# Products of ones ahead of the first rows, and a new order for the rest rows, the split rows and one weight's conversion

## The chip, the core and the metric

The kernel runs on one core of a Trainium2 chip. Its engines are TensorE (matrix products), VectorE and GpSimd (elementwise work), ScalarE (activation functions, copies, casts) and SyncE, whose queue issues the loads. In the rows of the profile they are called PE (PEld for its weight loads), DVE, POOL, ACT and SP. Each engine runs its instructions in a fixed order and waits where an input is missing or a buffer is not yet free. [...]

The metric is the device time of one execution in microseconds, as the median of several runs. Lower is better.

## What is computed

Four batches of 6336 rows and 256 channels go through channel attention and then a gated convolution:

```python
qn = q / (np.linalg.norm(q, axis=1, keepdims=True) + 1e-06)
kn = k / (np.linalg.norm(k, axis=1, keepdims=True) + 1e-06)
s = kn.transpose(0, 2, 1) @ qn / tau
a = softmax(s)                                  # 256 x 256 per batch
x = v @ a
gate = sigmoid(sum_k conv_w[k] * x shifted by k)    # 5 taps along the rows
out = (gate * (x @ w_val)) @ w_out
```

The softmax above stands for the reference's own lines (subtract the maximum, exponentiate, divide by the sum plus 1e-9). The weights w_val, conv_w and w_out arrive as 64-bit floating-point numbers, everything else as 32-bit ones.

## The kernel before

**Scores.** The sum k^T q runs over the 6336 rows of a batch. Rows are spread over the 128 partitions, 49 to a partition, so that a "row" of the kernel (one j) is 128 rows of the matrix; 64 rows remain, the *rest* (lines 47, 48). The 49 are cut into 17 groups: the first has one row, the others three (`GROUP`, lines 63 to 65). `load_group` (line 69) fetches a group of q and of k into one of six `raw` buffers; for the first group of each batch it also fetches the rest rows.

`score_group` (line 166) prepares a group and returns its products:

- A row with j below `nw` is *raw*: TensorE multiplies the 32-bit numbers as they are (line 222). A row from `nw` on is *split*: ScalarE casts it to a shorter format (line 192), GpSimd subtracts this from the original (line 193), and TensorE forms three products of the halves in the faster format for each half of the channels (line 224).
- The squares for the norms are formed by ScalarE (line 209, into `sq`, two buffers). VectorE adds the rows with j below `nv` to an accumulator in PSUM, GpSimd adds the others to one in SBUF (lines 210 to 214). The squares of a group stand behind that group's cast on ScalarE (line 196).

In batch 0 the first eleven groups are wholly raw, with two of the three rows added by VectorE; from group `SIDE` = 11 on, the third row is split and VectorE adds all three (line 172). In batch 1 the first five groups are raw, later ones are wholly split.

**The first loop** (lines 477 to 494) runs the 17 groups of batch 0. TensorE's first instruction is the product that clears the scores in PSUM (line 231), which needs the zeros that VectorE writes at line 88. At n = 6 it issues the loads of both weights (`load_weights`, line 105) and makes two generators, `prepare_weights(0)` for w_val with conv_w and `prepare_weights(1)` for w_out. Each turns the 64-bit words into 32-bit numbers in eight or more steps on VectorE (lines 132 to 154); for w_out ScalarE also makes a cast (line 149). From n = 9 on, two steps of each follow a group. The raw words of w_val take one of the three buffers of the split halves (tag `hi`), those of w_out one of the two output buffers (tag `o_sb`). At n = 13 the loads for batch 1's first groups and for the first rows of v follow.

**After it** (lines 495 to 524) the softmax of batch 0 goes on step by step (`softmax`, line 236, one step a `tick`). Between its steps TensorE works on batch 1's first five groups and transposes v; `behind` ties a block's instructions to stand behind a marked one of the same engine. Then comes the main loop over 52 steps of 508 rows of v: `conv` (product with the attention, five taps on ScalarE and VectorE), `sigmoid`, `value` (product with attention times w_val), `split_g` and `finish` (product with w_out, line 404, the first user of its two halves).

The order of the program's lines is a priority. The compiler decides each engine's order with it, and may put a later line ahead when the inputs of an earlier one are not there yet by its own estimate.

Of the kernel before, what the change touches and what calls it, by code (L numbers as in the profile page):

```python
# [17 lines left out]
P = 128  # L18
# [4 lines left out]
SIDE = 11  # L23
# [5 lines left out]
def kernel(  # L29
# [38 lines left out]

    def load_group(b, g):
        j0, n = groups[g]  # L70
        t = raw_p.tile([P, GROUP, 2, C], F32, name="raw")
        for s, src in ((0, q), (1, k)):
            main = src[b, 0:RP * P].rearrange("(p j) c -> p j c", j=RP)
            last_load[0] = nc.sync.dma_start(out=t[:, 0:n, s, :], in_=main[:, j0:j0 + n, :])  # L74
            if g == 0 and REST:
                nc.sync.dma_start(out=t[0:REST, n, s, :], in_=src[b, RP * P:N])
        raws[b, g] = t
# [10 lines left out]
    nc.vector.memset(zeros.bitcast(F32), 0.0)  # L88
    dummy = const.tile([P, 1], F32, name="dummy")
# [76 lines left out]
    def score_group(b, g):  # L166
# [4 lines left out]
        if b == 0:  # L171
            nw, nv = (GROUP, 2) if g < SIDE else (2, 3)
        else:
            nw, nv = (GROUP, 1 if g else 2) if b == 1 and g < LEAD else (0, 2)
        parts = [(P, 0, n)]
        if g == 0 and REST:
            parts.append((REST, n, 1))
# [10 lines left out]
        sq = split_p.tile([P, GROUP, 2, C], F32, name="sq", bufs=2)  # L188
# [21 lines left out]
        for np_, j in rows:  # L210
            if j in where:
                continue
            eng, key = (nc.vector, "acc") if j < nv else (nc.gpsimd, "side")
            eng.tensor_tensor(st[key][0:np_], st[key][0:np_], sq[0:np_, j], ALU.add)  # L214

        def mms(np_, j):
            r = slice(0, np_)
            stop = g == NG - 1 and np_ == parts[-1][0] and j == parts[-1][1] + parts[-1][2] - 1
            for h in range(NH):
# [5 lines left out]
                for n_, (lhs, rhs) in enumerate(ops):  # L225
                    nc.tensor.matmul(st["s"][:, h, :], lhs, rhs, start=False,  # L226
                                     stop=stop and h == NH - 1 and n_ == len(ops) - 1)
# [203 lines left out]
    marks = {}  # L431
# [41 lines left out]
    def step(n):  # L473
        return all_steps[n] if 0 <= n < len(all_steps) else None


    for n in range(NG):
        if n == 6:
            load_weights(0)
            load_weights(1)  # L480
            prep.extend(prepare_weights(part) for part in range(2))
        if n == NG - 4:
            load_upto(NG + 1)
            with tc.issue_after(last_load[0].ins):
                load_v(*step(0))
            load_upto(NG + 3)
# [3 lines left out]
        run_group()  # L490
# [28 lines left out]
    while stages:  # L519
        tick()  # L520
    for h in range(NH):
        transpose_v(*step(1), h)
# [84 lines left out]
```

## Time and profile before

| | us |
|---|---|
| median of 3 runs | 657.92 |
| fastest, slowest run | 657.75, 658.62 |
| span of the profiled execution, first to last instruction | 653.8 |

The profile gives no time of its own for the profiled execution beyond its span; the median of the runs is 4.1 us above it.

How it stands by stage, from the busy time by stretch (each entry is busy us of that stretch):

| stretch, us | what runs | TensorE | VectorE | ScalarE | GpSimd | GB/s |
|---|---|---|---|---|---|---|
| 0 to 14 | first loads, first groups | 10.55 | 4.14 | 6.97 | 2.21 | 259 |
| 14 to 38 | groups of batch 0 | 24.00 | 20.68 | 12.20 | 11.17 | 340 |
| 38 to 46 | groups of batch 0 | 6.44 | 7.65 | 5.44 | 3.74 | 327 |
| 46 to 54 | last groups of batch 0 | 8.00 | 7.41 | 6.10 | 3.86 | 279 |
| 54 to 72 | first softmax, batch 1's first groups | 17.33 | 10.79 | 12.16 | 5.62 | 345 |
| 72 to 82 | first steps of v | 8.68 | 8.58 | 9.08 | 9.12 | 216 |
| 82 to 100 | main loop | 18.00 | 15.39 | 14.02 | 16.09 | 232 |

A busy TensorE is not one at full pace: the ends of its products are modelled, and they overlap. Its pace is read from the distance between starts, or from the count of instructions in a stretch without idle time.

### The profile page before, as it was taken

To read this page: it belongs to the slowest core of one execution; us is meant where nothing else is said; L and a number is where in the kernel's file an instruction comes from. 1 tells how busy PE (TensorE), PEld (TensorE's weight loads), DVE (VectorE), ACT (ScalarE), POOL (GpSimd) and SP (SyncE) were. 2 spreads that over 40 slices of the span, in tenths; PEclk is the share of its full clock that TensorE was granted. 3 is DMA by queue.
4 is the path that set the end of the run, shared out by engine and by line. 5 is a ranking of instruction groups with operands and counts; after the bars stand their busy time and mean duration, and the time that the engine had idled before them with its cause. 6 is when DMAs were issued, how large, how long until landed. Compare 5 with 4: busy or idle time off the path is not lost.

```text
span 653.8 us, 10657 instructions
## 1 busy us (share of the span) xinstructions
PE 636.1 (97%) x4008; PEld 570.3 (87%) x4008; DVE 521.7 (80%) x831; ACT 465.7 (71%) x607; POOL 362.1 (55%) x174
## 2 busy tenths in 40 slices
PE   7999999999999999999998999999999999999996
PEld 5878799998979999999997998999999798988886
DVE  3897689787878688778788688778778889888894
ACT  5465978867888768668688787777777755655564
POOL 2441896965837769659565497766763122312221
PEclk9999999999999999999999999999999999999999
DMA  8999875555635665545554375653222343443213
GB/s 272 336 320 335 267 233 154 152 170 162 188 99 175 186 195 176 167 136 173 177 178 127 113 222 168 179 182 103 65 80 76 113 126 102 114 129 105 65 51 99
DMA packets 107875, 105.75 MB, mean 162 GB/s; under 512 B 5744, under 2 KB 107312, under 8 KB 107824
## 3 DMA queue, kind: packets, MB, share of 16 engines
q1 hardware_dynamic: 82048, 79.76, 39.8%
q10 hardware_dynamic: 25776, 25.32, 13.7%
q8 instruction: 31, 0.51, 0.3%
q14 instruction: 20, 0.16, 0.1%
HBM read 79.11 MB, written 25.95 MB: 161 GB/s over the span
## 4 chain that ended last, share of the span: by engine, by line
PE 84%; DVE 4%; ACT 4%; DMA 3%; SPq 2%; POOL 1%; issue 1%; ACTq 0%; DVEq 0%
PE o_ps L404 21%; PE x_ps L345 19%; PE val_ps L345 19%; PE s_ps L226 17%; PE t_ps L335 6%; SPq L74 2%; DMA raw<-in_k_dram 1%; PE o_ps L294 1%; POOL hi L193 1%; DMA w_raw<-in_moe_conv_w_dram 1%; DMA v_raw<-in_v_dram 1%; ACT hi L192 1%; DVE acc_ps L214 1%; DVE gate L361 1%; DVE gate L374 1%
## 5 line engine op out<-in xcount | busy, mean ns | idle before, releaser
L361 DVE SCALAR_TENSOR_TENSOR gate<-x_ps,wa,gate 128x508 f32<-128x508 f32 (+1 forms) x416 | 275.4, 718 | 14.4 <-ACT gate L359 13.4
L193 POOL TENSOR_TENSOR hi<-raw,hi 128x1536 fp32r<-128x1536 f32 (+2 forms) x54 | 167.8, 3109 | 92.8 <-ACT hi L192 92.8
L388 POOL TENSOR_TENSOR g_lo<-gate,g_hi 128x1016 fp32r<-128x1016 f32 (+1 forms) x50 | 116.8, 2335 | 145.1 <-ACT g_hi L387 130.5
L214 DVE TENSOR_TENSOR acc_ps<-acc_ps,sq 128x512 f32<-128x512 f32 (+1 forms) x134 | 93.5, 698 | 73.9 <-ACT sq L209 70.7
L345 PE MATMUL x_ps<-v_hi,w 128*128 128x512 f32 (+1 forms) x416 | 138.1, 391 | 0.0
L345 PE MATMUL val_ps<-v_hi,w 128*128 128x508 f32 (+1 forms) x416 | 133.9, 384 | 0.8 <-ACT o_sb L414 0.7
L226 PE MATMUL s_ps<-hi 128*128 128x256 f32 (+1 forms) x852 | 121.0, 287 | 6.2 <-ACT hi L192 4.0
L226 PEld LDWEIGHTS s_ps<-hi 128*128 128x128 f32 (+1 forms) x852 | 110.7, 190 | 12.6 <-ACT hi L192 5.5
L404 PE MATMUL o_ps<-wo_hi,g_hi 128*128 128x256 f32 x400 | 113.3, 283 | 0.2 <-DVE gate L374 0.2
L414 ACT COPY o_sb<-o_ps 128x512 f32<-128x512 f32 x99 | 58.1, 588 | 76.1 <-PE o_ps L404 74.8
L404 PE MATMUL o_ps<-wo_lo,g_hi 128*128 128x256 f32 x400 | 112.2, 281 | 0.0
L404 PE MATMUL o_ps<-wo_hi,g_lo 128*128 128x256 f32 x400 | 111.8, 280 | 0.0
L209 ACT ACTIVATE sq<-raw 128x1536 f32<-128x1536 f32 (+3 forms) x69 | 96.0, 1393 | 16.3 <-DVE acc_ps L214 8.0
L214 POOL TENSOR_TENSOR acc<-acc,sq 128x512 f32<-128x512 f32 x58 | 76.3, 1315 | 38.9 <-ACT sq L209 38.5
L345 PEld LDWEIGHTS val_ps<-v_hi,w 128*128 128x128 f32 x416 | 77.2, 188 | 14.4 <-ACT o_sb L414 0.9
L345 PEld LDWEIGHTS x_ps<-v_hi,w 128*128 128x128 f32 x416 | 77.5, 188 | 13.9 <-DVE gate L361 0.2
L359 ACT ACTIVATE gate<-x_ps,wa 128x508 f32<-128x508 f32 (+1 forms) x104 | 68.1, 669 | 20.6 <-PE x_ps L345 20.3
L336 ACT CAST v_hi<-t_ps 128x512 fp32r<-128x512 f32 (+1 forms) x104 | 55.7, 568 | 35.7 <-PE t_ps L335 33.2
L345 PE MATMUL x_ps<-v_lo,w 128*128 128x512 f32 (+1 forms) x208 | 79.8, 384 | 0.0
L345 PE MATMUL val_ps<-v_lo,w 128*128 128x508 f32 (+1 forms) x208 | 79.3, 381 | 0.0
L374 DVE TENSOR_TENSOR gate<-val_ps,gate 128x508 f32<-128x508 f32 (+1 forms) x104 | 64.3, 657 | 17.1 <-ACT gate L367 14.4
L404 PEld LDWEIGHTS o_ps<-wo_hi,g_hi 128*128 128x128 f32 x400 | 75.3, 188 | 1.4 <-DVE gate L374 0.4
(84 smaller groups left out, 800.0 us busy)
## 6 DMA issues: line engine op xcount, KB each, us to landing
raw<-in_q_dram SPq DMA_DIRECT2D x64, 384.0 KB
raw<-in_k_dram SPq DMA_DIRECT2D x64, 384.0 KB
v_raw<-in_v_dram SPq DMA_DIRECT2D x44, 512.0 KB
out_dram<-o_sb ACTq DMA_DIRECT2D x47, 384.0 KB
out_dram<-o_sb ACTq DMA_DIRECT2D x47, 124.0 KB
v_raw<-in_v_dram SPq DMA_DIRECT2D x4, 384.0 KB
raw<-in_q_dram SPq DMA_DIRECT2D x4, 128.0 KB
raw<-in_k_dram SPq DMA_DIRECT2D x4, 128.0 KB
```

What stands on the lines that cost most here:

```text
L193: nc.gpsimd.tensor_tensor(hi[r, js, :, 1, :], raw[r, js, :, :], hi[r, js, :, 0, :].bitcast(F32), ALU.subtract)
L209: nc.scalar.activation(sq[0:np_, ja:jb], raw[0:np_, ja:jb], AF.Square)
L214: eng.tensor_tensor(st[key][0:np_], st[key][0:np_], sq[0:np_, j], ALU.add)
L226: nc.tensor.matmul(st["s"][:, h, :], lhs, rhs, start=False, stop=stop and h == NH - 1 and n_ == len(ops) - 1)
L336: nc.scalar.copy(th[:, h, 0:w], tp[:, 0:w])
L345: marks["PRODUCT"] = nc.tensor.matmul(ps, wt[:, which, ws, ch, hs], vs[:, ch, lo:hi_], start=n_ == 0, stop=n_ == 3 * NH - 1)
L359: nc.scalar.activation(gate[:, h, 0:w], x_ps[:, 0:w], AF.Copy, scale=cw[:, h, 0:1])
L361: nc.vector.scalar_tensor_tensor(gate[:, h, 0:w], x_ps[:, tap:tap + w], cw[:, h, tap:tap + 1], gate[:, h, 0:w], ALU.mult, ALU.add)
L374: nc.vector.tensor_tensor(gate[:, h, 0:w], val_ps[:, 0:w], gate[:, h, 0:w], ALU.mult)
L388: nc.gpsimd.tensor_tensor(gl[:, :, 0:w], gate[:, :, 0:w], gh[:, :, 0:w].bitcast(F32), ALU.subtract)
L404: nc.tensor.matmul(o_ps[:, u * C:(u + 1) * C], gs[:, h, off:off + P], ws[:, h, :], start=n_ == 0, stop=n_ == 3 * NH - 1)
L414: marks["ACT"] = nc.scalar.copy(o_sb[:, j:j + len(pair), :], o_ps[:, 0:len(pair) * C].rearrange("p (j c) -> p j c", c=C))
```

## The change

Four things change, all in the part before the main loop.

1. Ten products of a 128 x 128 block of ones with itself, into a PSUM bank that nobody reads (`spin`): six ahead of the first clear, four behind the products of group 0 of batch 0. Groups 0 and 1 are tied to stand behind them.
2. In batch 0 the 64 rest rows are fetched with, and belong to, the group with index 3 (`REST_AT`), not the first. `raw` and `sq` get room for a fourth row; the rest's squares are always added by VectorE.
3. In batch 0 the groups up to index 3 are raw; from index 4 (`FIRST_SPLIT`) on, the third row of every group is split, and VectorE adds two rows in groups of even index and three in those of odd index.
4. w_val's load and conversion are set up at n = 5 instead of 6. w_out's load follows that of the first rows of v, at n = 13, and its conversion stands behind the last step of the first softmax.

```diff
-SIDE = 11
+REST_AT = 3
+FIRST_SPLIT = 4
...
+    def rest_of(b, g):
+        return REST if g == (0 if b else REST_AT) else 0
+
     def load_group(b, g):
...
-        t = raw_p.tile([P, GROUP, 2, C], F32, name="raw")
+        t = raw_p.tile([P, GROUP + 1, 2, C], F32, name="raw")
...
-            if g == 0 and REST:
+            if rest_of(b, g):
...
+    warm = ps.tile([P, 512], F32, name="warm", tag="bank")
+
+    def spin(n):
+
+        for _ in range(n):
+            marks["SPIN"] = nc.tensor.matmul(warm[:, 0:P], ones, ones, start=True, stop=True)
+
+    marks = {}
+    spin(6)
...
         if b == 0:
-            nw, nv = (GROUP, 2) if g < SIDE else (2, 3)
+            if g < FIRST_SPLIT:
+                nw, nv = GROUP + 1, 2
+            else:
+                nw, nv = GROUP - 1, 2 + g % 2
...
-        if g == 0 and REST:
+        if rest_of(b, g):
             parts.append((REST, n, 1))
...
-        sq = split_p.tile([P, GROUP, 2, C], F32, name="sq", bufs=2)
+        sq = split_p.tile([P, GROUP + 1, 2, C], F32, name="sq", bufs=2)
...
-            eng, key = (nc.vector, "acc") if j < nv else (nc.gpsimd, "side")
+            eng, key = (nc.vector, "acc") if j < nv or np_ < P else (nc.gpsimd, "side")
...
     for n in range(NG):
-        if n == 6:
+        if n == 5:
             load_weights(0)
-            load_weights(1)
-            prep.extend(prepare_weights(part) for part in range(2))
+            prep.append(prepare_weights(0))
         if n == NG - 4:
             load_upto(NG + 1)
             with tc.issue_after(last_load[0].ins):
                 load_v(*step(0))
+                load_weights(1)
...
-        run_group()
+        with behind(*(["SPIN"] if n < 2 else [])):
+            run_group()
+        if n == 0:
+            with behind("SCORES"):
+                spin(4)
...
     while stages:
         tick()
+    for _ in prepare_weights(1):
+        pass
     for h in range(NH):
         transpose_v(*step(1), h)
```

`marks["SCORES"]` is the last score product issued so far, `marks["SPIN"]` the last product of ones.

More of the change, by code (lines that the diff above doesn't have):

```diff
@@ L225, in mms @@
                 for n_, (lhs, rhs) in enumerate(ops):
-                    nc.tensor.matmul(st["s"][:, h, :], lhs, rhs, start=False,
-                                     stop=stop and h == NH - 1 and n_ == len(ops) - 1)
+                    marks["SCORES"] = nc.tensor.matmul(st["s"][:, h, :], lhs, rhs, start=False,
+                                                       stop=stop and h == NH - 1 and n_ == len(ops) - 1)
         def clear():
@@ L430 @@
     stages, prep = [], []
-    marks = {}
     @contextmanager
```

## The prediction

> **What bounds the kernel now.** I read the page first, then TensorE's timeline over batch 0's scores (0 to 55 us), then the busy time by stretch, then the timelines of ScalarE, VectorE and the DMA queue there.
>
> ```profile
> span 653.8 us, 10657 instructions
> ...
> PE 636.1 (97%) x4008; PEld 570.3 (87%) x4008; DVE 521.7 (80%) x831; ACT 465.7 (71%) x607; POOL 362.1 (55%) x174
> ...
> PE 84%; DVE 4%; ACT 4%; DMA 3%; SPq 2%; POOL 1%; issue 1%; ACTq 0%; DVEq 0%
> ```
>
> TensorE holds 84% of the chain that ends last. What it gains early therefore stays gained unless a later stage takes it back. The change lies almost wholly in the first 55 us, so the question is what TensorE loses there.
>
> ```profile
> 1.60 0.80 PE L231 MATMUL s_ps<-zeros 128*128 128x512 f32 x1 [1.60 <-DVE zeros L88]
> ...
> 4.25 26.01 PE L226 MATMUL s_ps<-raw 128*128 128x256 f32 x96 [1.85 <-DMA raw<-in_k_dram]
> ...
> 8.22 21.85 PEld L226 LDWEIGHTS s_ps<-raw 128*128 128x128 f32 x89 [0.65 <-issue]
> ...
> 8.22 5.49 PE L226 MATMUL s_ps<-raw 128*128 128x256 f32 x12
> ...
> 13.91 22.40 PE L226 MATMUL s_ps<-raw 128*128 128x256 f32 x103
> ...
> 39.22 0.86 PE L226 MATMUL s_ps<-hi 128*128 128x256 f32 x5 [0.21 <-POOL hi L193]
> ...
> 42.17 0.38 PE L226 MATMUL s_ps<-hi 128*128 128x256 f32 x1 [0.38 <-ACT hi L192]
> 43.54 0.86 PE L226 MATMUL s_ps<-hi 128*128 128x256 f32 x5 [0.98 <-POOL hi L193]
> 44.23 1.89 PE L226 MATMUL s_ps<-raw 128*128 128x256 f32 x8
> 45.77 1.06 PE L226 MATMUL s_ps<-hi 128*128 128x256 f32 x6
> 46.67 1.89 PE L226 MATMUL s_ps<-raw 128*128 128x256 f32 x8
> ...
> 54.83 0.50 PE L231 MATMUL s_ps<-zeros 128*128 128x512 f32 x1 [0.67 <-DMA v_raw<-in_v_dram]
> ```
>
> The columns are start, length, what, count and the idle time before. Three things are to be seen.
> - **Pace.** From 13.91, 103 raw instructions take 22.40 us: 0.216 each without the last one's tail (two instructions a product). A raw group of three rows is 12 of them, 2.59 us. From 8.22, 12 take 5.49: about 0.43 each, half the pace. So the array ran slow until 13.91.
> - **Split groups.** From 44.23 to 46.67 a group with two raw rows and one split row takes 2.44 us: 8 x 0.216 = 1.73, and 0.71 for six split products. A split row saves 0.15 us.
> - **Stalls.** Between 39 and 44 us TensorE waits for the split row's halves, in two groups. The first loses at least the 0.21 at 39.22; from there to the same product of the next group (43.54) are 4.32 us instead of 2.44, 1.88 lost: 2.1 in all.
>
> Undisturbed from 44.23, batch 0 ends four groups later, at 44.23 + 4 x 2.44 = 54.0.
>
> ```profile
> 34.85 1.48 ACT L209 ACTIVATE sq<-raw 128x1536 f32<-128x1536 f32 x1 [3.44 <-DVE acc_ps L214]
> ...
> 40.95 0.66 ACT L149 CAST wo_hi<-w_raw 128x512 fp32r<-128x512 f32 x1 [2.47 <-DVE w_raw L146]
> ...
> 41.51 0.61 ACT L192 CAST hi<-raw 128x512 fp32r<-128x512 f32 x1
> ```
> ```profile
> 22.00:41.00 19.00, 18.79 (x91) 16.41 (x90) 18.78 (x28) 7.99 (x7) 7.71 (x6) 1.00 1.09 351
> ...
> 22.00:41.00 19.00, 5.65 (x9) 0.00 (x0) 1.00 1.09 351
> ```
>
> The stalls come from VectorE. In 22 to 41 us it is busy 18.78 of 19 us (third pair of the first row), and the sums of squares (second row, the acc_ps tile alone) are only 5.65 of that. The other 13.1 us convert the two weights: about 6 for w_val and 7 for w_out. ScalarE stands behind it, so the cast for a split comes late.
>
> **The change, part by part.** *Products of ones.* No row shows such a product of 128 columns; two kinds bound it, the raw instruction and the transpose.
>
> ```profile
> 60.75 1.04 PE L335 MATMUL t_ps<-ident,v_raw 128*128 128x128 f32 x8
> ...
> L335 PE MATMUL t_ps<-ident,v_raw 128*128 128x128 f32 x392 | 54.2, 273 | 0.4 <-DVE gate L374 0.4
> ```
>
> Eight transposes of 128 columns take 1.04 us, and without the last one's 0.27 seven steps take 0.77: 0.11 each. The raw instruction with 256 columns takes 0.216. At half pace that is 0.22 to 0.43; I take 0.22, the row with as many columns. Six products are 12 instructions: 2.7 us, from about 1.1 (ones are written before the zeros, which end by 1.60) to 3.8, and the clear follows by 4.25, when the first row started anyway. At 0.43 each group 1 would begin some 2 us later, of which 1.1 would be left beside the waits for data charged below. Row 0 takes 4 x 0.43 = 1.7, to about 5.9, and the four further products 8 x 0.22 = 1.8, to 7.7, or less when the pace has risen by then. In the trace the pace rose 5.7 us after the last pause of the weight loads (8.22 to 13.91). In the changed kernel the array is busy from 1.1 with no break, so the same delay gives 6.8. Then the 13 slow instructions up to 13.91 take 13 x 0.216 = 2.8 instead of 5.7: **2.9 us gained**.
>
> [...]
>
> *Rest rows.* Their two loads leave the head of the queue.
>
> ```profile
> 1.21 0.55 SPq L76 DMA_DIRECT2D raw<-in_q_dram  x1
> ...
> 2.43 0.48 SPq L76 DMA_DIRECT2D raw<-in_k_dram  x1
> ...
> 7.67 0.63 ACT L205 ACTIVATE acc<-raw 128x512 f32<-128x512 f32 x1 [1.94 <-DMA raw<-in_k_dram]
> ```
>
> Each costs the queue about 0.6 us with its gap, so group 1, which landed just before 7.67, lands at about 6.5. TensorE begins it at about 7.2 (between 6.5 and 7.7), 1.0 us before the 8.22 of now. The rest's four slow instructions went where TensorE waited for data; in the fourth group they cost 4 x 0.216 = 0.86 us, with one more square on ScalarE and one more sum on VectorE.
>
> *Split rows.* Groups 4 to 10 turn from 2.59 to 2.44: 7 x 0.15 = **1.0 us**. The prices of the helpers:
>
> ```profile
> L192 ACT CAST hi<-raw 128x512 fp32r<-128x512 f32 x8 | 4.8, 606 | 0.0
> ...
> L209 ACT ACTIVATE sq<-raw 128x1536 f32<-128x1536 f32 x60 | 89.2, 1487 | 15.2 <-DVE acc_ps L214 7.2 <-DMA raw<-in_k_dram 4.2 <-DVE w_raw L134 3.0
> ...
> L193 POOL TENSOR_TENSOR hi<-raw,hi 128x512 fp32r<-128x512 f32 x8 | 10.5, 1309 | 6.2 <-ACT hi L192 6.2
> ...
> L214 DVE TENSOR_TENSOR acc_ps<-acc_ps,sq 128x512 f32<-128x512 f32 x130 | 90.7, 698 | 69.0 <-ACT sq L209 66.4
> ...
> L214 POOL TENSOR_TENSOR acc<-acc,sq 128x512 f32<-128x512 f32 x58 | 76.3, 1315 | 38.9 <-ACT sq L209 38.5
> ```
>
> For each 2.44 us group ScalarE needs 0.61 + 1.49 = 2.1, GpSimd 1.31 for the split and 1.31 more in every second group, VectorE two or three sums of 0.70. All fit. w_val's raw words take one of the three split buffers until converted; with two left, a cast waits for the products two groups back, so it starts 2.44 us before its group, and cast plus subtraction (1.9) are done before the split row's turn. w_val's load, issued a group earlier, shifts one group's landing by its 1.5 us (in the sum of the data below). No other cost.
>
> *TensorE's own path:* 7.2 + two raw groups 5.2 + the fourth with the rest 3.45 + 13 x 2.44 = 31.7 gives 47.5, against 54.0: at most 6.5 us (2.9 pace, 2.1 stalls, 1.0 earlier start, 1.0 splits, less rounding and the rest row now in the path).
>
> *The data* do not come 6.5 us earlier.
>
> ```profile
> 19.00:22.00 3.00, 3.00 (x16) 2.64 (x15) 1.93 (x3) 1.48 (x1) 2.03 (x2) 1.00 1.17 258
> ...
> 22.00:45.00 23.00, 21.44 (x103) 18.36 (x102) 22.47 (x33) 11.99 (x11) 9.90 (x8) 1.00 1.09 350
> ...
> 45.00:54.00 9.00, 9.00 (x54) 8.19 (x52) 8.37 (x14) 7.01 (x8) 4.25 (x4) 1.00 0.94 269
> ...
> 54.00:72.00 18.00, 17.33 (x87) 14.60 (x86) 10.79 (x19) 12.16 (x20) 5.62 (x4) 1.00 1.07 345
> ...
> 72.00:82.00 10.00, 8.68 (x46) 6.60 (x45) 8.58 (x14) 9.08 (x12) 9.12 (x7) 1.00 0.69 216
> ```
>
> The last column is GB/s. At 350 a group (786 KB) takes 2.25 us. From group 1 at 6.5 to the last: 15 x 2.25 = 33.7, rest rows 0.4, w_val 1.5, the slow stretch at 19 to 22 (conv_w's small packets) 0.8: 42.9, or 44 with 1 us for hitches. The last group still needs cast, subtraction and products, about 2.6: 45.5 to 47. So data are just ahead of TensorE, with 0.4 us to spare at group 7 (7.2 + 8.65 + 3 x 2.44 = 23.2 against 6.5 + 6 x 2.25 + 2.7 = 22.7). I add 1.0 us for groups that wait: 48.5, **5.5 us gained**.
>
> *VectorE* still converts w_val in this stretch, 6 us between sums that take 1.8 of each 2.44. Six groups (14.6 us) hold 15 sums (10.5 us) and the conversion: it falls 2 to 3 us behind, and a cast stands behind a square that waits for the sums two groups earlier. The cost is between 0 and the whole lag of 2.7; the split row's turn comes 1.73 us after its group's start, which covers most of it: I take 0.7.
>
> *w_out behind the first softmax.* Its load (1.5 us) now stands between batch 1's first groups; 45 to 54 at 269 GB/s leaves room (9 us x 81 GB/s = 0.73 MB). Its 7 us on VectorE and the cast of 0.66 on ScalarE go to 50 to 85 us. VectorE is idle 18.00 - 10.79 = 7.2 us in 54 to 72, in gaps; in 72 to 82 only 1.4. Nothing needs w_out before its first product at 96.20:
>
> ```profile
> 96.20 0.28 PE L404 MATMUL o_ps<-wo_hi,g_hi 128*128 128x256 f32 x1
> ```
>
> ScalarE's cast waits for eight pieces before it, and all of ScalarE's squares and taps queue behind it, as for 2.47 us at 40.95. Hidden in those gaps it costs nothing; with the whole 7 us in front of the weights' low half (L299) or the taps (L361) it costs up to 7. The gaps lie among the softmax's steps, and a piece of 0.4 to 1.8 us in front of such a step delays it. I take 0.7. A further 0.5 goes to batch 1's raw groups, whose data come at 345 GB/s already.
>
> **Sum:** 5.5 - 0.7 - 0.7 - 0.5 = 3.6 us. The profiled span becomes 650.2. The median run, 657.92, is 4.1 us over that span, which I leave as it is: **654.3 us**.
>
> **The rivals.** *All hidden.* TensorE's own path is the bound, and w_out lies in the gaps: 6.5 less 0.3, 651.7. For it: data and TensorE are near each other. Against: the margin of 0.4 us at group 7. Chance 0.10.
>
> *The pace does not rise sooner*: products of ones do not count for it, so the change does not do what it says. Then groups 1 and 2 up to 13.91 run slow, and the path is 7.7, then 14.5 instructions to 13.9, 9.5 x 0.216 = 2.1, 3.45 and 31.7: 51.2, 2.8 gained, less 0.7: 655.8. Against it: what raised it now was unbroken work of the same kind. Chance 0.13.
>
> *VectorE takes TensorE's place*: more split rows wait for a late cast, since w_val's conversion now falls among split groups. Its price, 2.7 us more than none, leaves 5.5 - 2.7 - 1.2 = 1.6: 656.3. For it speak two rows of one operation, and GpSimd's row beside the first:
>
> ```profile
> L146 DVE TENSOR_TENSOR w_raw<-w_raw,wa 128x522 int32<-128x522 int32 x1 | 1.6, 1619 | 0.0
> ...
> L146 DVE TENSOR_TENSOR w_raw<-w_raw,wb 128x512 int32<-128x512 int32 x1 | 0.7, 674 | 0.0
> ...
> 29.33 1.27 POOL L214 TENSOR_TENSOR acc<-acc,sq 128x512 f32<-128x512 f32 x1 [2.12 <-ACT sq L209]
> ```
>
> 1.62 against 0.67 us for one operation; the long one (from 29.56) ran beside that sum of GpSimd's, the short one beside none, and GpSimd will be busier. [...] Chance 0.18, half of it within 0.2%.
>
> *w_out in the wrong place* (the slower side). The order that the compiler gives the engines puts all pieces on VectorE directly in front of L299, in the stretch where it has 1.4 us of 10 to spare and GpSimd is busy 9.12. TensorE's value products then wait 7 to 8 us more, less the 1.4. It decides where this wait passes the 4.8 us gained before it: 7.5 - 1.4 - 4.8 = 1.3, about 660 with the softmax and the next taps late by 0.8. For it: the conversion stands there in program order. Against: VectorE's pieces were placed among the sums wherever it had room, and room comes earlier. Chance 0.14, of which 0.02 within 0.2%.
>
> **How the numbers follow.** The forecast (own range 653.0 to 655.5) has 0.45. A measurement here can tell about 0.2%, 1.3 us. Faster: 0.45 + 0.10 + 0.13 + 0.09 = 0.77. Within: 0.09 + 0.02 = 0.11. Slower: 0.12. The range runs from 651.6 (all hidden) to 657.6 (VectorE's rival with the upper price of a product of ones, 1.1 us more); what is left out is the slower rival and half of the best one.
>
> **What would show it.** Raw instructions at 0.216 from about 7 us; no second stretch of half pace; the second clear (now 54.83) near 50; split rows waiting under 1 us in all; the DMA at 350 GB/s until 50 us; VectorE's pieces of w_out between 54 and 72; the first L404 near 92.6. The prediction is wrong if raw instructions stay at 0.43 past 8 us, if ScalarE waits for sums ahead of casts in most groups, or if TensorE idles over 2 us before the value products of the first step.

## The result, and the profile after

| | before | after |
|---|---|---|
| median of 4 runs each, side by side, us | 658.27 | 653.71 |
| fastest, slowest | 657.75, 659.03 | 652.86, 654.47 |
| span of the profiled execution | 653.8 | 651.0 |
| time of a run less its span | 1.9 (first experiment) | 1.86 |

The ratio is 0.9935 (95% interval 0.9919 to 0.9950): about 4.3 us gained, where 654.3 us had been forecast against a kernel before of 657.92. The two profiled spans differ by only 2.8 us. Why the runs differ by more than the two profiles is the question of the first experiment.

The page after: busy times, and the chain that ended last, shared out by engine.

```profile
PE 634.7 (97%) x4042; PEld 570.8 (88%) x4042; DVE 519.5 (80%) x831; ACT 469.6 (72%) x614; POOL 370.7 (57%) x181
...
PE 80%; DMA 6%; ACT 6%; DVE 3%; POOL 2%; issue 2%; SPq 1%; ACTq 0%; POOLq 0%
```

TensorE is busy for 1.4 us less than before, VectorE for 2.2. TensorE still has most of the chain, but 80% instead of 84: the DMA has 6 instead of 3, ScalarE 6 instead of 4. So some of the work that the change takes off TensorE's path has been replaced by waits.

TensorE's timeline over batch 0 (start, length, what, count, idle time before and its releaser; the kernel's lines from the score products on stand 16 lower in the file than before, so the clear is L247, the score products L242, the norms L261):

```profile
1.06 2.93 PE L98 MATMUL warm<-ones 128*128 128x128 f32 x12 [1.06 <-DVE ones L90]
...
7.03 2.83 PE L242 MATMUL s_ps<-raw 128*128 128x256 f32 x12 [0.31 <-DMA raw<-in_k_dram]
10.70 8.47 PE L242 MATMUL s_ps<-raw 128*128 128x256 f32 x36 [0.84 <-DMA raw<-in_k_dram]
...
32.42 1.97 PE L242 MATMUL s_ps<-raw 128*128 128x256 f32 x8 [0.35 <-DMA raw<-in_k_dram]
...
37.55 0.86 PE L242 MATMUL s_ps<-hi 128*128 128x256 f32 x5 [0.42 <-POOL hi L209]
...
42.89 0.85 PE L242 MATMUL s_ps<-hi 128*128 128x256 f32 x5 [0.20 <-POOL hi L209]
...
50.23 1.06 PE L242 MATMUL s_ps<-hi 128*128 128x256 f32 x6
52.17 0.70 PE L261 MATMUL o_ps<-acc_all,ones 128*128 128x256 f32 x2 [0.87 <-DVE acc_all L256]
...
53.89 0.47 PE L247 MATMUL s_ps<-zeros 128*128 128x512 f32 x1
```

- **The pace** rose early: 12 raw instructions of group 1 take 2.83 us from 7.03 (0.23 each), where the kernel before needed 5.49 from 8.22.
- **The data** did not come earlier with it. Group 2 waits 0.84 us, and starts at 10.70. By the prediction's group lengths, counted from group 1's start, batch 0 would end near 47.5; it ends at 51.3 (50.23 and 1.06), 3.8 us later. By the distances of the groups' starts, some 2.0 us of this lie at group 2, just behind it and around 32.42 us, 1.1 at the two waits for the split halves, the rest in smaller gaps and the last product's tail.
- **The order** behind batch 0 is another one. Before, TensorE cleared batch 1's scores and did eight raw products ahead of the norms (clear at 54.83, norms at 57.18). Now the norms come first, and wait 0.87 us for the sum acc_all.

The stretch in which VectorE converted both weights, by busy time (us, then busy time and count of TensorE, its weight loads, VectorE, ScalarE and GpSimd, the clock, the DMA's share, GB/s):

```profile
22.00:41.00 19.00, 18.24 (x103) 16.09 (x102) 17.17 (x25) 13.13 (x14) 13.54 (x11) 1.00 1.04 314
```

VectorE has 1.8 us to spare there, where before it had 0.2; ScalarE and GpSimd, with a split in every group, have become busier by 5 to 6 us. The data run at 314 GB/s, where before it was 351; why is not shown.

The wait for acc_all has a cause that the prediction did not have, on VectorE's timeline:

```profile
47.32 3.71 DVE L230 TENSOR_TENSOR acc_ps<-acc_ps,sq 128x512 f32<-128x512 f32 x5
51.09 0.43 DVE L145 TENSOR_SCALAR wb<-w_raw 128x512 int32<-128x512 int32 x1
51.43 0.68 DVE L256 TENSOR_TENSOR acc_all<-acc_ps,acc 128x512 f32<-128x512 f32 x1
```

VectorE's sums end at 51.0, and the first piece of w_out's conversion (L145) stands ahead of acc_all (L256). Here it delays acc_all by 0.34 us (51.09 to 51.43); in the fifth experiment it is seen waiting there for w_out's load. Further on the two profiles run in parallel: the first x_ps product is 2.71 us earlier than before, every product of the main loop 2.53, the first product with w_out among them:

```profile
93.67 0.28 PE L420 MATMUL o_ps<-wo_hi,g_hi 128*128 128x256 f32 x1
```

It stood at 96.20. Where a profile stands against the kernel before at this product (its **lead**, 2.53 here) is a good measure for what follows: in the kernels whose engines have the same order in the main loop, a lead stays what it is until something new happens. In five kernels (experiments 2, 4, 7, 8 and 10) the compiler gave VectorE and ScalarE another order in the main loop, though nothing was changed there; what that costs is seen in experiment 2.

### The profile page after: what moved, and what is told of

It is laid out like the page before. It is cut to its first block, busy times and chain, and to the rows that moved or that the text cites. A ratio compares the mean times of both kernels' runs of the same rounds, so it can differ in the third digit from the quotient of the medians.

```text
span 651.0 us, 10754 instructions
## 1 busy us (share of the span) xinstructions
PE 634.7 (97%) x4042; PEld 570.8 (88%) x4042; DVE 519.5 (80%) x831; ACT 469.6 (72%) x614; POOL 370.7 (57%) x181
## 4 chain that ended last, share of the span: by engine, by line
PE 80%; DMA 6%; ACT 6%; DVE 3%; POOL 2%; issue 2%; SPq 1%; ACTq 0%; POOLq 0%
PE o_ps L420 20%; PE val_ps L361 19%; PE x_ps L361 19%; PE s_ps L242 14%; PE t_ps L351 6%; DMA raw<-in_k_dram 3%; DMA raw<-in_q_dram 1%; ACT sq L225 1%; POOL acc L230 1%; DMA w_raw<-in_moe_w_out_dram 1%; SPq L78 1%; PE o_ps L310 1%; DMA out_dram<-o_sb 1%; POOL hi L209 1%; ACT gate L383 1%
## 5 line engine op out<-in xcount | busy, mean ns | idle before, releaser
L209 POOL TENSOR_TENSOR hi<-raw,hi 128x1536 fp32r<-128x1536 f32 (+2 forms) x61 | 177.5, 2912 | 91.9 <-ACT hi L208 91.8
L242 PE MATMUL s_ps<-hi 128*128 128x256 f32 (+1 forms) x894 | 128.9, 288 | 5.6 <-ACT hi L208 3.7
L242 PEld LDWEIGHTS s_ps<-hi 128*128 128x128 f32 (+1 forms) x894 | 116.6, 190 | 12.6 <-ACT hi L208 4.7
L208 ACT CAST hi<-raw 128x1536 fp32r<-128x1536 f32 (+2 forms) x61 | 75.2, 1238 | 5.2 <-DMA raw<-in_k_dram 3.2
```

The lines of the kernel that those rows point to most:

```text
L208: cast = nc.scalar.copy(hi[r, js, :, 0, :], raw[r, js, :, :])
L209: nc.gpsimd.tensor_tensor(hi[r, js, :, 1, :], raw[r, js, :, :], hi[r, js, :, 0, :].bitcast(F32), ALU.subtract)
L242: marks["SCORES"] = nc.tensor.matmul(st["s"][:, h, :], lhs, rhs, start=False, stop=stop and h == NH - 1 and n_ == len(ops) - 1)
```

## The experiments

Each ratio is to the kernel before on the same chip, with its 95% interval.

| kernel | ratio | lead in its profile, us |
|---|---|---|
| the change, first runs | 0.9935 (0.9919 to 0.9950) | 2.53 |
| the change, again | 0.9946 (0.9929 to 0.9964) | 0.80 |
| the kernel before, again | 1.0004 (0.9991 to 1.0017) | -0.83 |
| change without the products of ones | 0.9958 (0.9942 to 0.9975) | 3.05 |
| before with the products of ones alone | 1.0017 (1.0003 to 1.0032) | -1.15 |
| change with w_out among the scores | 1.0029 (1.0017 to 1.0042) | -2.66 |
| before with w_out's move alone | 0.9999 (0.9984 to 1.0014) | -0.60 |
| change with the rest rows first | 0.9957 (0.9944 to 0.9970) | 1.56 |
| change with split rows from group 11 | 1.0010 (0.9998 to 1.0023) | -0.44 |
| the same with the change's shares of the sums | 0.9978 (0.9963 to 0.9993) | 2.09 |
| change, w_out's pieces behind acc_all | 0.9948 (0.9929 to 0.9968) | 2.59 |
| the same, w_val earlier and spread | 0.9944 (0.9924 to 0.9963) | 3.88 |
| the same, a pause near 354 us filled | **0.9916 (0.9901 to 0.9930)** | 4.18 |

**1. The kernel before, again.**

> The kernel before, unchanged, to have the span beside the time of each of its runs. The two profiled spans differ by 2.8 us (653.8 and 651.0), the two medians by 4.6 (658.27 and 653.71); every run of the changed kernel took 1.86 us more than its span. If the rest of the difference is the moment at which the pace of TensorE rises (it varies from run to run without the products of ones, and the profiled execution had an early one), the runs here have spans of 655.9 to 657.2, time less span is 1.9 again, and the profile taken now may show the rise later than 13.9 us. Rival: time less span is about 4.1 us for this kernel, and spans are near 653.8 in every run; then 1.8 us of the gain lie outside the span.

In its 12 runs the time less the span is 1.9 us in each (658.11 against 656.2, 656.02 against 654.1), and the spans reach from 654.1 to 657.1. The profile of before, at 653.8, was thus one of the quickest executions of its kernel, and its rival (4.1 us outside the span) falls. But the pace rose as early as in the first profile: group by group the two agree up to 38 us. Two other things differ. This one is 0.83 us behind by the end of batch 0, in the waits at the first split groups, and then loses 1.61 us at one place far behind the change. TensorE's timeline there:

```profile
357.74 0.39 PE L226 MATMUL s_ps<-hi 128*128 128x256 f32 x1 [2.69 <-ACT hi L192]
...
359.24 0.63 PE L345 MATMUL x_ps<-v_lo,w 128*128 128x512 f32 x1
359.67 1.06 PE L345 MATMUL x_ps<-v_hi,w 128*128 128x512 f32 x2
```

and the same stretch by busy time (busy us and count of TensorE, its granted clock, then the DMA's share and GB/s), first in the first profile of before, then in this one:

```profile
357.00:361.00 4.00, 4.00 (x19) 1.00 0.33 83
```
```profile
357.00:361.00 4.00, 3.27 (x10) 0.68 0.47 130
```

TensorE waits 2.69 us for a cast of ScalarE. That pause stands in both profiles, and in every other one of this study, at the same place of the program. Here the products behind it start 0.43 us apart instead of 0.23 for some 3 us; in the first profile they do not. The granted clock of 0.68 is a mean over the 4 us; over the next four (361 to 365) it is 0.89. In 9 of the 13 profiles up to the last experiment the clock falls so around or after this pause; the four without are the two first profiles (before and after), that without products of ones and that with the rest rows first. So the first pair of profiles were both lucky there. Filling the pause is the last experiment.

The mean granted clock that is on record beside each run answers the question of this experiment. Of the 91 runs of the kernel before in this study, 31 have a mean of 0.999, as an execution without a fall, and spans with a median of 654.1 us; the other 60 have 0.992 to 0.997 and a median of 655.85. Of the ten runs of the change, seven have 0.999 or 1.000 and a median span of 651.3 us, three have 0.996 or 0.997 and 652.4 to 654.3. Among executions without a fall the gain is thus 2.8 us, as in the two profiles. Most of what the medians show beyond it comes from the change's runs having met fewer falls, and no run shows that the change makes them rarer: in its variants of experiments 9 and 11, four runs of six have one.

**2. Without the products of ones.**

```diff
-    spin(6)
...
-        with behind(*(["SPIN"] if n < 2 else [])):
-            run_group()
-        if n == 0:
-            with behind("SCORES"):
-                spin(4)
+        run_group()
```

> The changed kernel without the ten products of ones; rest rows, split rows and w_out stay as changed. Theory (each part pays some of it, the early pace is capped by the landings of the data): the rise comes back to 11 to 14 us, TensorE's end of batch 0 moves from 51.1 to between 52.0 and 53.5, time 655 to 656.3, that is 1.3 to 2.6 us lost. Rival 1 (the gain is the pace alone): time 657.5 to 658.5, as the kernel before. Rival 2 (the data and VectorE set the end of batch 0 whatever the pace): 653.4 to 654.3, nothing lost, with fewer waits after 20 us.

Measured 0.9958, 654.42 us. Of TensorE's timeline:

```profile
6.68 13.44 PE L240 MATMUL s_ps<-raw 128*128 128x256 f32 x48 [1.11 <-DMA raw<-in_k_dram]
...
50.32 1.06 PE L240 MATMUL s_ps<-hi 128*128 128x256 f32 x6
52.07 0.70 PE L259 MATMUL o_ps<-acc_all,ones 128*128 128x256 f32 x2 [0.69 <-DVE acc_all L254]
```

48 raw instructions at full pace would be 10.4 us; they take 13.44, so 3 us go to the slow start. Yet batch 0 ends where it ended with the products of ones (51.4 and 51.3), the norms start within 0.1 us, and the lead is even 0.5 us larger. TensorE, being late, finds its data there: no wait between 6.68 and 42 us. What the early pace brings in batch 0 comes back as waits, as rival 2 has it. The ratio is 0.0012 to 0.0023 worse than with them, and all these intervals overlap.

What may be left of a difference, 0 to 1.5 us, does not come from the products of ones in batch 0. This profile loses 1.4 us of its lead near 363 us, without a fall of the clock:

```profile
363.57 0.43 PE L349 MATMUL t_ps<-ident,v_raw 128*128 128x128 f32 x2 [1.15 <-DVE gate L388]
```
```profile
360.22 2.71 DVE L375 SCALAR_TENSOR_TENSOR gate<-x_ps,wa,gate 128x508 f32<-128x508 f32 x4
```

VectorE takes four taps ahead of the product that TensorE waits for; in the change it takes two there (1.39 us from 360.74). This is the other order of the five kernels named above. In the four others a fall of the clock lies at this place and the loss behind it is 1.4 to 1.65 us in all, so that what the order alone costs is shown by this one profile. The second group's k landed at 9.25 us here and at 10.56 in the changed kernel, so a part of what that profile lost was a late transfer; whether the products of ones bring that is taken up below.

**3. The products of ones alone** (all other parts of the diff undone).

> The kernel before plus the products of ones only (rest rows in group 0, split rows from the twelfth group, both weights converted among the scores as before). Theory: the raw products from group 1 on run fast from about 7 us, but VectorE's 13 us of conversion still end at the same time, so the stalls at 39 to 44 us grow by most of what the pace brings; time 656.5 to 657.8, 0.5 to 1.8 gained. Rival 1 (the pace alone is the gain): 653.5 to 654.5. Rival 2 (the products of ones bring nothing): 658 or more.

Measured 1.0017, 658.28 us: no gain at all, the interval just on the slower side. The theory's 0.5 to 1.8 us did not come; by the time it is rival 2.

```profile
8.24 18.30 PE L242 MATMUL s_ps<-raw 128*128 128x256 f32 x84
27.59 2.86 PE L242 MATMUL s_ps<-raw 128*128 128x256 f32 x12 [1.06 <-DMA raw<-in_k_dram]
31.18 7.14 PE L242 MATMUL s_ps<-raw 128*128 128x256 f32 x32 [0.73 <-DMA raw<-in_k_dram]
...
41.66 0.38 PE L242 MATMUL s_ps<-hi 128*128 128x256 f32 x1 [0.90 <-ACT hi L208]
43.02 0.97 PE L242 MATMUL s_ps<-hi 128*128 128x256 f32 x5 [0.97 <-POOL hi L209]
43.78 3.50 PE L242 MATMUL s_ps<-raw 128*128 128x256 f32 x8
```

The products run at full pace from 8.24, then wait for data twice and for the split halves twice, where before had only the latter. And behind these pauses eight raw instructions take 3.50 us instead of 1.89: the pace falls here too. So the products of ones do bring the early pace (rival 2 has the time, not the reason), but here the head start of TensorE over VectorE and the data is paid back in pauses, and behind them the pace fell.

**4. w_out among the scores again**, all else as changed.

```diff
             load_weights(0)
-            prep.append(prepare_weights(0))
+            load_weights(1)
+            prep.extend(prepare_weights(part) for part in range(2))
...
-                load_weights(1)
...
-    for _ in prepare_weights(1):
-        pass
```

> The changed kernel with w_out loaded and converted among the scores of batch 0 again (both weights from the sixth group on); all else as changed. Theory: VectorE has 7 us more in 27 to 51 us, where it already ran late in the changed kernel (w_val's pieces of 1.1 to 1.2 us beside GpSimd); split rows wait for casts, batch 0 ends 2 to 5 us later, time 655.5 to 658.5. Rival 1 (the pace alone is the gain): within 0.5 us of 653.7. Rival 2 (w_out was the whole gain): 657.5 or more, with waits at split rows of 3 us or more in all and no change before 30 us.

Measured 1.0029, some 6 us slower than the change, above what the theory gave and in the range of rival 2; that w_out's move is the whole gain, as rival 2 has it, experiment 8 refutes.

```profile
38.40 0.39 PE L242 MATMUL s_ps<-hi 128*128 128x256 f32 x1 [1.20 <-ACT hi L208]
39.75 0.86 PE L242 MATMUL s_ps<-hi 128*128 128x256 f32 x5 [0.96 <-POOL hi L209]
...
42.73 0.39 PE L242 MATMUL s_ps<-hi 128*128 128x256 f32 x1 [0.39 <-ACT hi L208]
44.52 1.01 PE L242 MATMUL s_ps<-hi 128*128 128x256 f32 x5 [1.41 <-POOL hi L209]
45.33 3.45 PE L242 MATMUL s_ps<-raw 128*128 128x256 f32 x8
```

3.96 us of waits on the split halves and 1.56 us for the slow eight behind them: 5.5, against a loss of 5.2 in the lead (2.53 to -2.66). So the split rows in every group cannot bear both conversions beside them.

**5. The change, again.**

> The changed kernel, unchanged, with five rounds beside its variants. If the products of ones pay (theory 1, the prediction's), the ratio to before is 0.9935 again and 0.2% under that without them (0.9958). If they pay nothing because data or VectorE set the end of batch 0 (theory 2, which the first four runs favour: batch 0 ended at 51.3 us with them and at 51.4 without), the spans without a stretch of half pace later are 650.5 to 651.5 and the ratio is 0.994 to 0.996. The second group's k landed at 10.56 us in the first profile and at 9.25 in that without the products of ones: a landing near 9.3 here says that the delay was chance, one near 10.5 that the products bring it.

Measured 0.9946, five of six spans between 651.1 and 652.1; the profiled one, 654.3, is the odd one, and shows the new wait at its worst. TensorE, then VectorE:

```profile
50.80 1.06 PE L242 MATMUL s_ps<-hi 128*128 128x256 f32 x6
53.89 0.70 PE L261 MATMUL o_ps<-acc_all,ones 128*128 128x256 f32 x2 [2.03 <-DVE acc_all L256]
```
```profile
52.81 0.43 DVE L145 TENSOR_SCALAR wb<-w_raw 128x512 int32<-128x512 int32 x1 [1.23 <-DMA w_raw<-in_moe_w_out_dram]
53.15 0.68 DVE L256 TENSOR_TENSOR acc_all<-acc_ps,acc 128x512 f32<-128x512 f32 x1
```

VectorE stands idle for 1.23 us before a piece of w_out whose load is late, acc_all stands behind it, and TensorE behind that. The theory that the products of ones pay gives a ratio 0.2% under that without them; it is 0.12% under, within the interval of both, and 0.9946 lies in the range of the theory that they pay nothing. Group 2's k landed by 10.10 us here, between the two values that were to tell chance from the products of ones; TensorE waited 0.75 us for it.

**6. The rest rows first** (`REST_AT = 0`), all else as changed.

> The changed kernel with batch 0's rest rows back in the first group (REST_AT = 0). By the prediction's working, group 1 then starts at 8.2 instead of 7.0 and the 0.86 us of the rest's products move out of TensorE's path: 0.2 to 1.0 us slower. Rival: where the data set the pace, the same bytes pass the queue in either order; the end of batch 0 stays within 0.4 us of 51.3 and the time within 0.5 us of the changed kernel's.

Measured 0.9957, 654.38 beside 653.22 for the change on the same chip: 0.0011 in ratio, within the intervals. Group 1 starts at 8.19 as worked out, and batch 0 ends at 52.3, 1.0 later than in the first profile of the change and 0.4 later than in the second. The prediction's 0.2 to 1.0 us and the rival's 0.5 both include it; this part is small, and not settled more closely.

**7. Split rows only from group 11**, all else as changed (`FIRST_SPLIT = 11`, and VectorE takes all three sums from there on, as before).

> The changed kernel with split rows from the twelfth group only, as before (groups 4 to 10 are raw). By the prediction's working 7 x 0.15 = 1.0 us slower, less the waits for data that the slower products cover: 0 to 1.0 slower. Rival: the splits bring more waits on casts and on GpSimd's subtraction than they save, VectorE's pieces beside GpSimd's subtractions being longer: 0.3 to 1.0 us faster, w_val's pieces shorter (0.5 to 0.9 us) and no wait on hi before 38 us.

Measured 1.0010: both were wrong. Undoing this part, priced at 1.0 us, takes away the whole gain.

```profile
50.21 1.06 PE L242 MATMUL s_ps<-hi 128*128 128x256 f32 x6
53.86 0.70 PE L261 MATMUL o_ps<-acc_all,ones 128*128 128x256 f32 x2 [2.59 <-DVE acc_all L256]
...
54.76 1.87 PE L351 MATMUL t_ps<-ident,v_raw 128*128 128x128 f32 x8
```

TensorE ends batch 0 at 51.27, as in the change. But VectorE has three sums in each of the last groups, acc_all ends late, TensorE pauses for 2.59 us, and the eight transposes behind take 1.87 us instead of 1.07: the pace fell. The norms are 1.69 us later than in the change, and the first x_ps product 3.35 (70.39 against 67.04). Such falls are the rule with this kernel: its twelve runs all have a mean clock of 0.996 or less.

**8. w_out's move alone** (all other parts of the diff undone).

> The kernel before with only w_out's load and conversion moved behind the first softmax (no products of ones, rest rows in the first group, split rows from the twelfth group). By the prediction's working this gives the 2.1 us of the stalls less 0.7 less 0.5: 0.9 us, ratio 0.9985. Rival, from the run with w_out early (6 us slower than the changed kernel): the move is the main part of the change, 2.5 to 4 us, ratio 0.994 to 0.9962; no wait on hi at the first two split groups, batch 0 ends at 51.0 to 52.0.

Measured 0.9999: no gain seen, though the theory's 0.9985 lies within the interval; the rival's range does not. The rival's signs in the trace did come, with no wait at the first split groups, and batch 0 ending at 51.5, 2.7 us earlier than before. Then the same as in the run before:

```profile
50.42 1.06 PE L240 MATMUL s_ps<-hi 128*128 128x256 f32 x6
53.70 0.78 PE L259 MATMUL o_ps<-acc_all,ones 128*128 128x256 f32 x2 [2.21 <-DVE acc_all L254]
```

Runs 3, 7, 4 and the change itself make a table of two by two, with products of ones in each: neither part 1.0017, w_out's move only 1.0010, split rows only 1.0029, both 0.9935 and 0.9946. By time the gain belongs to the pair. The table is not quite clean: run 3 has its rest rows first (worth 0.0011 at most by experiment 6), and runs 4 and 7 have the costlier order of the main loop (up to 1.4 us, 0.0021); neither makes up the 0.0064 to 0.0094 between them and the change. What the pair does: the move takes 7 us off VectorE ahead of the end of batch 0; the other sharing of the sums lets VectorE finish them in time for the norms, which the move has brought to the front.

**9. w_out's pieces behind acc_all**, all else as changed: `marks["ACC"]` is the sum acc_all, and

```diff
-    for _ in prepare_weights(1):
-        pass
+    with behind("ACC"):
+        for _ in prepare_weights(1):
+            pass
```

> The changed kernel with the pieces of w_out's conversion queued behind the sum acc_all on VectorE; otherwise the same. Theory: w_out's first piece stands ahead of acc_all and waits for w_out's load (1.23 us in one profile), and TensorE's norms wait for acc_all (0.87 and 2.03 us in the two profiles of the changed kernel). Behind it the wait before the norms falls to 0.7 us or less in every run; 0.3 to 1.5 us gained on the changed kernel, ratio to before 0.992 to 0.9942. Rival: VectorE's own sums end so late that acc_all is not earlier; ratio 0.994 to 0.996 and a wait before the norms of 0.8 us or more.

Measured 0.9948. The wait before the norms falls to 0.51 us, as the theory has it; but the ratio shows no gain. It lies in the rival's range, and its interval, 0.0039 wide, covers most of the theory's too, so on the time nothing is settled. The lead, 2.59, was reached although the granted clock was 0.95 all through this one execution (the 56 raw instructions of batch 1 take 13.12 us instead of 12.64); its span, 653.8, is not to be compared.

**10. Raw rows, but the sums shared as in the change.** From run 7's kernel: `nw = GROUP + 1 if g < 11 else GROUP - 1`, and `nv = 2 if g < 4 else 2 + g % 2`.

> The changed kernel with groups 4 to 10 raw, as before, but with the sums of squares shared between VectorE and GpSimd as in the changed kernel (VectorE two, then three, in turn from group 4 on). With raw rows and the old sharing the time was the kernel before's again (1.001), though TensorE ended batch 0 at the same 51.3 us: it then waited 2.59 us for acc_all. Theory (the sharing of the sums is what the split edit brings): acc_all is in time, the wait before the norms is 1 us or less, ratio 0.994 to 0.997. Rival (the split rows themselves are what brings it, through TensorE's shorter groups or the casts): ratio 0.999 or more, as in that run.

Measured 0.9978, between theory and rival.

```profile
7.17 29.50 PE L240 MATMUL s_ps<-raw 128*128 128x256 f32 x132
...
48.51 1.06 PE L240 MATMUL s_ps<-hi 128*128 128x256 f32 x6
50.57 0.70 PE L259 MATMUL o_ps<-acc_all,ones 128*128 128x256 f32 x2 [1.00 <-DVE acc_all L254]
```

The sharing alone takes 1.6 us off the wait before the norms and brings the lead from -0.44 to 2.09. It moves sums, and adds none: in both kernels VectorE adds 32 rows from group 4 on, here three of them earlier, so that the last six groups hold 15 instead of 18. TensorE even ends batch 0 at 49.6, 1.7 us earlier than with split rows, and waits for nothing there: raw rows need no cast, so none is late. What it gains is lost again, 1.3 us between the norms and the first x_ps product (0.53 of it for batch 1's data) and more at the first steps of v (0.85 us for a copy of ScalarE ahead of the product with w_val).

By the lead it is 0.4 us behind the change, by time 2 us. Two things on record bear on the rest. Seven of its twelve runs have a mean clock of 0.996 or less, three of the change's ten 0.997 or less. And its other order of VectorE can take its share where the clock does not fall: its five runs at 0.998 have spans of 652.7 to 655.2 us, the change's seven without a fall 651.0 to 652.1. How the 2 us divide stays open.

**11. w_val earlier and spread**: from run 9's kernel, `n == 3` for its load, and one piece a group from n = 6 on.

> The changed kernel with w_out's pieces behind acc_all, w_val's load two groups earlier (n == 3) and its conversion from the seventh group on, one piece a group. Theory (VectorE's lag from w_val sets the late casts of groups 11 to 14): the waits on hi between 36 and 45 us (0.6 to 1.3 us in all in the two profiles) go, batch 0 ends at 49.5 to 50.8, 0.5 to 1.5 us faster than the changed kernel with only w_out's pieces moved. Rival 1 (the data set the end, the last group landing near 47 to 48 us): waits on hi turn into waits on data, no gain, within 0.4 us. Rival 2: w_val's load, now among the first groups' data, delays TensorE where it has no margin: 0.5 to 1.5 us slower.

Measured 0.9944 against 0.9948. The waits on the split halves do not go but move to the new place of the conversion (0.42, 0.22 and 0.94 us between 31 and 39 us). Batch 0 ends at 51.5, so the theory missed; the time is rival 1's, but its mechanism did not come, since no wait turned into one for data. Acc_all is in time:

```profile
50.43 1.06 PE L242 MATMUL s_ps<-hi 128*128 128x256 f32 x6
51.33 0.59 PE L261 MATMUL o_ps<-acc_all,ones 128*128 128x256 f32 x2
```

The lead is 3.88, the best so far; but in this profile the clock falls at the pause near 354 us, and the lead falls to 2.53. Group 2 does not wait for data here, with products of ones, and landed at 9.6 or earlier in run 9 too. Against 10.1 in run 5 and 10.56 in the first profile, this says that the landing varies from one execution to the next and that the products of ones need not make it late.

**12. The pause filled.** From run 11's kernel: eight products of ones behind the last product of `finish` (`marks["FINISH"]`), in an otherwise untouched order.

```diff
+        if n == 23:
+            warm = ps.tile([P, 512], F32, name="warm", tag="bank")
+            with behind("FINISH"):
+                spin(8)
...
             if turn == 0:
-                run_group()
+                with behind(*(["SPIN"] if n == 24 else [])):
+                    run_group()
```

> The previous variant (w_out's pieces behind acc_all, w_val earlier, one piece a group) plus eight products of ones in a pause that stands in every profile of this case near 354 us (2.69 us, TensorE waits for ScalarE's cast of a split group); nothing else in any engine's order is changed. In 9 of 13 profiles, that variant's among them, TensorE's granted clock falls to 0.6 to 0.86 in the 4 us around or after that pause and the products run at half pace, which costs 1.4 to 1.7 us; in the others it doesn't. Theory (the pause is what brings it, and its chance phase is what spreads the runs): the pause shrinks to about 1.5 us or is cut in two, the clock stays 1.00 there, the profile's later milestones keep the 3.9 us that it is ahead of the kernel before, most spans lie at 649.8 to 650.6, ratio 0.991 to 0.993. Rival 1 (the fall of the clock has another cause, the heat or the time since the start): spans spread as before, 651 to 653.3, ratio 0.993 to 0.996. Rival 2 (the products start late, after ScalarE's copy frees their bank, and push the group behind them): the group starts up to 1 us later and the ratio is no better.

Measured 0.9916, median 651.54 us beside 657.74: the quickest kernel of the study. TensorE's timeline, and its busy time around:

```profile
350.87 2.05 PE L98 MATMUL warm<-ones 128*128 128x128 f32 x16 [0.84 <-ACT o_sb L430]
352.73 0.39 PE L242 MATMUL s_ps<-hi 128*128 128x256 f32 x1
```
```profile
349.00:353.00 4.00, 3.16 (x27) 1.00 0.50 175
353.00:357.00 4.00, 4.00 (x20) 1.00 0.28 67
```

The products start 0.84 us into the pause, when ScalarE's copy frees their bank, and end when the cast is done; the group behind them is not late. The clock stays at 1.00, the lead stays 4.18 to the end, and all five spans lie between 649.6 and 650.7. The same kernel without them had 651.0 to 653.3 in six runs. All five have a mean clock of 0.998 or 0.999, as executions without a fall. With the pause filled none of the five runs shows a fall, where four of run 11's six do. The median is 1.8 us lower than in run 11 (the intervals of the two ratios still overlap by 0.0006; the spans do not). The falls are not the whole of it: two of run 11's six runs have none either (0.999) and took 651.0 and 651.8 us. The two kernels ran on different chips, and what makes the rest is not shown.

## Why the prediction was right, and where not

The time was right (654.3 for 653.71), the range and the side too. The working was not right in all its steps, two of its errors took each other away, and the number owes something to luck: the forecast gained 3.6 us, executions without a fall of the clock gain 2.8, and the 4.6 us between the medians came about with the help of falls that the change's runs did not meet.

- **Pace.** Forecast: the rise at 6.8 us. Products of ones do count: the distance of raw instructions falls from 0.43 to 0.22 at 5.4 us. The rival in which they don't falls. In the ten profiles with them group 1's products, the first of which starts between 6.46 and 8.24 us, run at 0.22 to 0.24 us an instruction. Of the four without, before has 5.49 us for the first 12 from 8.22, and run 2 takes 13.44 us for 48.
- **What the pace is worth** is the step that failed. "5.5 us gained" at the end of batch 0, after 1.0 for groups that wait for data, and 0.7 less for VectorE's lag, were 2.86 (the last six split products start at 50.23 instead of 53.09). The waits and gaps take 3.8 us, not 1.7: some 2.0 for data where 1.0 was summed, at 314 GB/s and not 350, and 1.1 to 1.3 behind late halves where 0.7 was. The kernel without products of ones ends batch 0 at the same time. The prediction had the margin of data and TensorE in its hands (0.4 us at group 7) and still credited most of the 2.9 us. (Its 6.5 us for TensorE's own path is right by the path, 54.0 less 47.5; the four parts that it names for it, less the 0.86 of the rest rows, add up to only 6.1.)
- **Splits and stalls.** The stalls of 2.1 us at the first two split groups went (idle times of 0.42 and 0.20 us are left at groups 11 and 13). But 1.0 us for seven split rows was the wrong term: run 10 has raw rows and ends batch 0 earlier. Undoing the whole edit costs some 4 us; in its place run 10 shows when VectorE adds its sums, costed at nothing under "all fit": all but 0.4 us of it by the lead, about half by the time. How the other half divides between falls of the clock and the other order of VectorE is open.
- **w_out's move.** Its pieces lie between 51 and 62 us (54 to 72 in the forecast), in gaps, and TensorE needs 14.9 us from the norms to the first x_ps (52.17 to 67.04), as many as before from the clear (54.83 to 69.75). So the 0.7 for the gaps and the 0.5 for batch 1's data were not lost there. Lost instead were 0.87 us at the norms, for a reason the prediction did not name: VectorE's sums end late, and a piece of w_out, which may still wait for its load, stands ahead of acc_all. It asked who waits behind ScalarE's cast, not who waits behind VectorE's first piece. The rival with all pieces in front of L299 did not come.
- **The second clear** (forecast near 50, now 53.89) and the **first product with w_out** (92.6, now 93.67) show the two last points: the norms went ahead of the clear, and 1.1 us less was gained than summed.
- **Span and time.** A net 3.6 us were forecast for the span; the two profiles differ by 2.8. But the 4.1 us between span and median, "which I leave as it is", were 1.9 us outside the span and 2.2 us of a profile that was quicker than the runs. The changed kernel's profile was quick too, its median only 0.85 us above it. A span 0.8 us longer than forecast and a level 1.4 us lower (653.71 against 651.0 + 4.1 = 655.1) make the 0.6 us by which the forecast was off.

## What to carry to other kernels

Three engines ran level in this stage, and neither of the two main parts that were run alone (products of ones, w_out's move) showed a gain: relieve all that end together, and ask what the relief brings to the front of the queue (here the norms) and what that waits for. Before reading a difference of 3 us out of two profiles, read the spans and clocks of many runs of one kernel: here they differ by as much. See, too, whether the compiler has kept the order in stages that were not touched. And look at the pace behind a pause of TensorE: here one of 2.69 us was followed by a fall in most profiles, which cost 1.35 to some 1.6 us beside the pause. With products on dummy data in it (run 12) the group behind was not late, and the clock stayed at 1.00.

## What the runs showed of the hardware

**Behind a pause of TensorE the pace fell in most profiles.** The gap of 2.69 us (2.64 in run 9) near 354 us was followed by a fall in 9 of 13 profiles; in run 1 products behind it start 0.43 us apart instead of 0.23. Behind gaps of 2.59 and 2.21 us in runs 7 and 8 eight transposes took 1.87 and 1.95 us instead of 1.07; behind one of 2.03 us in run 5 they took 1.07. In runs 3 and 4 the pace fell behind pairs of shorter gaps (0.90 and 0.97 us, 0.39 and 1.41): eight raw instructions took 3.50 and 3.45 us instead of 1.89. The falls near 354 us cost 1.35 (run 11) to some 1.6 us (run 1) each; run 9, whose clock was 0.95 throughout, is left out here.

**The same gap did it in some executions and not in others.** Over 357 to 361 us the granted clock was 1.00 in four profiles (the first of before and of the change, runs 2 and 6) and between 0.58 (run 3) and 0.85 (run 10) in eight others; run 11's fall came earlier (0.76 over 350 to 357 us). Run 12, with products of ones in the gap, has 1.00 from 349 to 361 us. What decides in which execution the clock falls is not shown.
